# Loading a head's query and key stacks in eight transfers instead of twelve, and passing the row maxima through DRAM in three transfers instead of eight

## The chip, the cores and the metric

The kernel runs on one core of a Trainium2 chip. The metric is the device time of one execution in microseconds (us). Three runs of the kernel before took 3000.59, 3006.46 and 3000.59 us, a median of 3000.59 us.

## The reference: what is computed

Two multi-head attention blocks, A and B, read the same input `x` of 2048 tokens by 512 features. Each has 32 heads of 16 features, a full softmax over 2048 keys and an output projection. A gate per token mixes the two results.

```python
x = A_x
g = _sigmoid((x * gate_w).sum(-1, keepdims=True))
a = _A_ref(x, A_wqkv, A_wo)      # qkv projection, softmax(q k^T / 4) v per head, output projection
b = _B_ref(x, B_wqkv, B_wo)
return g * a + (1 - g) * b
```

So there are 64 heads in all (32 of A, then 32 of B), each with a 2048 by 2048 score matrix.

## The kernel before, in words

**Precision.** TensorE works on a rounded 32-bit type. To keep accuracy, a value is split into a rounded part ("hi") and the rest ("lo"), and a product is made from hi·hi + lo·hi + hi·lo. For the scores this is done by stacking: for head h, the tile `k_st` holds the 16 key rows as hi, lo, hi (48 partitions), and `q_st` holds the query rows as hi, hi, lo. One matrix product over these 48 partitions sums the three terms. Two more partitions of `q_st` (rows 48 and 49 of the stack) hold the row maximum of every query, split in two parts, and the same rows of `k_st` hold -1, so a product over 50 partitions gives score minus maximum. The whole stack is there twice, at partitions 0 and 64 (`HALVES`), so that two matrix products with different row groups can run side by side.

**Prologue** (about the first 304 us). The projections to q and k (`project_qk`, L192 to L199) write both parts of q and k of each group of eight heads to DRAM tensors `qd` and `kd` of shape [2 parts, 8 heads, 16, 2048]. `project_v` (L214 to L218) writes v to DRAM. The stacks of heads 0 and 1 are loaded here by the GpSimd (POOL) queue.

**Main loop** (L552 to L577). It has 1024 rounds: 64 heads of 16 key tiles of 128 keys. A round r of head h has two halves. In each half, TensorE makes:

- two score products of 128 keys by 512 queries (`scores`, L540), which ScalarE (ACT) turns into exponentials (L543);
- two products for the row maxima of a later head (`max_half`, L108), which VectorE (DVE) reduces over 1024 keys (L110); these are 20 rounds ahead of the scores (16 rounds and `LEAD` = 4);
- eight products with v for the round before (`attend`, L512), which add up in PSUM.

When the last maximum of a head is done (round 16h - 5), `max_split` joins the two half maxima (L120 on VectorE) and splits them in two parts on GpSimd (L121, L122). One round later (round 16h - 4), `max_rows` transposes the small tile in blocks of 32 by 32 on VectorE (L127, tile `mt`, 128 partitions of 32 values), and the SyncE (SP) queue carries it into rows 48 and 49 of both stacks of `q_st` (L131). Round 16h, the first round of head h, needs these rows.

`load_stacks(h + 2)` is issued on the SP queue at the start of round 16h (L559, L95, L96), into the buffer that head h - 1 has just finished with (three buffers). The first maximum products that read it are those of round 16h + 12.

Where a head ends, its sums leave PSUM through ScalarE (L529) and the SP queue (L530). After each group of eight heads the results are normalised and projected (`load_den` to `project_out`, L344 to L400), spread over the rounds of the next group by a table of due rounds (`at`, L452 to L497). The order of the work on each engine is the order of the program text; `tc.manual_schedule()` keeps it, and the framework adds the semaphore waits that the tiles' reads and writes need.

Of the kernel before, what the change touches and what calls it, by code (L numbers as in the profile page):

```python
# [23 lines left out]
F32 = mybir.dt.float32  # L24
# [9 lines left out]
S = 2048  # L34
DM = 512
H = 32
DH = 16
# [4 lines left out]
HG = H // NG  # L42
# [6 lines left out]
SC = 3 * DH  # L49
# [3 lines left out]
def gated_mha(ctx: ExitStack, tc: tile.TileContext, xT, x, wqkv_a, wo_a, wqkv_b, wo_b, gate_w, out):  # L53
    nc = tc.nc
# [6 lines left out]
    dram = ctx.enter_context(tc.tile_pool(name="dram", bufs=1, space=DRAM))  # L61
# [3 lines left out]
    kd = [[dram.tile([2, HG, DH, S], F32, name=f"kd{s}{g}") for g in range(NG)] for s in range(2)]  # L65
    vd = [dram.tile([S, H * 17], F32, name=f"vd{s}") for s in range(2)]
    od = [dram.tile([HG, NQ, 32, 512], F32, name=f"od{g}") for g in range(2 * NG)]
    rd = [dram.tile([HG, S], F32, name=f"rd{g}") for g in range(2 * NG)]

    ident = const.tile([P, P], BF, name="ident")  # L70
# [14 lines left out]
    def load_stacks(h, dma=None):  # L85
        dma = dma or nc.sync.dma_start
        s, hh = divmod(h, H)
        g, j = divmod(hh, HG)
        q, k = q_st[h % 3], k_st[h % 3]
        qs, ks = qd[s][g], kd[s][g]  # L90

        for b in HALVES:
            for i in range(3):
                r = slice(b + i * DH, b + (i + 1) * DH)
                dma(k[r].bitcast(F32), ks[i % 2, j])  # L95
                dma(q[r].bitcast(F32), qs[i // 2, j])  # L96

    mxp = {}

# [25 lines left out]
    def max_rows(h):  # L125
        mt = small.tile([P, 32], F32, name="mt")
        dve.transpose(mt, mparts.pop(h).rearrange("p i t -> p (i t)").bitcast(F32))  # L127
        q = q_st[h % 3]
        for b in HALVES:
            for a in range(4):  # L130
                nc.sync.dma_start(  # L131
                    q[b + SC:b + SC + 2].bitcast(F32).rearrange("i (t a x) -> i t a x", a=4, x=32)[:, :, a],
                    mt[32 * a:32 * a + 32])


    vpool = ctx.enter_context(tc.tile_pool(name="vpool", bufs=2))
# [10 lines left out]
    with tc.tile_pool(name="xs", bufs=1) as xs, tc.tile_pool(name="pro", bufs=2) as pro, \  # L147
# [98 lines left out]
        for i, (s, g, isk) in enumerate(blocks):  # L246
            block(split_w, i + 1)
            block(load_w, i + 3)
            if i in (2, 8):
                load_w(i // 8, 2 * DM, DM)  # L250
            if i in (4, 9):
                split_w(i // 8, 2 * DM, DM)
            project_qk(s, g, isk, lambda: run_ahead(i >= 10))
            if i in (7, 9):
                load_stacks((i - 7) // 2, pool.dma_start)
            if i == 7:
                for t in range(NT):
                    project_v(0, t)
            if i == 9:
                for c in range(4):  # L260
                    load_v(0, c)
        for t in range(NT):
            project_v(1, t)
            if pending:
                pending[0] += 1
                if pending[0] == 3:
                    max_rows(pending.pop() - 3)
            if t:
                run_ahead(2)
# [282 lines left out]
    for r in range(ROUNDS + 1):  # L552
        for fn, a in later.pop(r, ()):
            fn(*a)
        h, kt = divmod(r, NT)
        m = r + NT + LEAD
        if r < ROUNDS:
            if kt == 0 and h + 2 < NH:
                load_stacks(h + 2)  # L559
            pt[r] = ppool.tile([P, S], F32, name="p")  # L560
            for half in range(2):
                pair(r, (2 * half, 2 * half + 1))
                if m < ROUNDS:
                    max_half(m, half)
                elif fill and r >= fill[0][0]:
                    fill_in(r)
                if r:
                    attend(r - 1, half)
            if m < ROUNDS and m % NT == NT - 1:
                max_split(m // NT)  # L570
                after[r + 1] = m // NT
        else:
            attend(r - 1, 0)
            attend(r - 1, 1)
        if r in after:
            max_rows(after.pop(r))
        fill_in(r)  # L577
# [27 lines left out]
```

## Time and profile before

| | before |
|---|---|
| median of three runs | 3000.59 us |
| profiled execution | 3003.09 us |
| its span, first to last instruction | 3001.3 us |
| granted TensorE clock, mean | 0.994 |
| TensorE (PE) busy | 2962.8 us, 99% |
| VectorE (DVE) busy | 2678.3 us, 89% |
| ScalarE (ACT) busy | 2336.4 us, 78% |
| GpSimd (POOL) busy | 206.1 us, 7% |
| share of the chain that ended last on PE | 93% |
| transfers of `k_st` and `q_st` loads on the SP queue | 372 and 372, 128 KB each |
| transfers of `mt` into `q_st` on the SP queue | 512, 4 KB each |

The span is the time from the first to the last instruction. "Busy" counts the time in which an engine's instructions are recorded as running; matrix products overlap each other, so a PE that is always busy may still be held up, and the distance between the starts of two instructions says more than their durations. In the timeline a row gives start, duration, engine, line, operation, tile written and tiles read, shape and count. Transfers are issued by a queue (SPq, POOLq) and land later; a row's duration is that of issuing.

### The profile page before, as it was taken

What the parts mean: (1) busy time and instruction counts of PE and PEld (TensorE: products, weight loads), DVE (VectorE), ACT (ScalarE), POOL (GpSimd) and SP (SyncE); (2) the same over time, 40 slices, a digit from 0 to 9 for tenths busy, and PEclk for the clock granted to TensorE, in tenths of its full rate; (3) what the DMA queues carried; (4) which work ended last, traced back from release to release, by engine and by line L of the source; (5) the groups of instructions that cost most, each with busy time, mean ns of one, the idle gap of its engine ahead of it and who ended that gap; (6) DMA issues with size and microseconds to landing.
All of it is one profiled execution on the core that took longest, in us unless ns stands there. A gap on an engine that the chain in (4) does not pass through costs nothing.

```text
span 3001.3 us, 62628 instructions
## 1 busy us (share of the span) xinstructions
PE 2962.8 (99%) x26192; PEld 1207.5 (40%) x26192; DVE 2678.3 (89%) x2423; ACT 2336.4 (78%) x4277; POOL 206.1 (7%) x325
## 2 busy tenths in 40 slices
PE   8999999999999999999999999999999999999998
PEld 6877333333333333333333333333333333333334
DVE  3135999999999999999999999999999999999974
ACT  3221888888788878888788878888788878888893
POOL 2000222001000100001000100000000100000000
PEclk9999999999999999999999999999999999999998
DMA  8453444333333423343234432343334443343302
GB/s 254 184 199 120 79 76 77 55 60 53 56 59 52 77 41 54 55 81 48 44 55 66 66 53 40 55 81 51 53 47 63 65 62 47 45 76 51 55 12 81
DMA packets 94162, 213.65 MB, mean 71 GB/s; under 512 B 34552, under 2 KB 44760, under 8 KB 81592
## 3 DMA queue, kind: packets, MB, share of 16 engines
q1 hardware_dynamic: 90552, 197.58, 36.8%
q0 software_dynamic: 3328, 12.06, 1.4%
q8 instruction: 207, 3.39, 0.5%
q14 instruction: 75, 0.61, 0.1%
HBM read 143.78 MB, written 63.69 MB: 69 GB/s over the span
## 4 chain that ended last, share of the span: by engine, by line
PE 93%; ACT 3%; DMA 2%; issue 1%; DVE 0%; SPq 0%; ACTq 0%; DVEq 0%
PE acc L512 36%; PE ps_st L540 29%; PE ps_mx L108 16%; PE ps_pro L192 5%; PE ps_mx L395 4%; PE ps_pro L214 3%; ACT p L543 2%; ACT ev L529 1%; DMA q_st<-qd 1%; DMA qd<-part 1%; DMA kd<-part 0%; PE ps_mx L445 0%; DMA raw<-in_xT 0%; ACT o_hi L383 0%; DMA rb<-rd 0%
## 5 line engine op out<-in xcount | busy, mean ns | idle before, releaser
L543 ACT ACTIVATE p<-ps_st 128x512 f32<-128x512 f32 x4096 | 2223.5, 596 | 411.8 <-PE ps_st L540 189.3
L110 DVE TENSOR_REDUCE mxp<-ps_mx 128x1 f32<-128x1024 f32 x2048 | 2486.8, 1222 | 61.9 <-PE ps_mx L108 54.4
L512 PE MATMUL acc<-p,vg 128*17 128x256 f32 x16384 | 1287.5, 386 | 12.7 <-ACT ev L529 11.4
L540 PE MATMUL ps_st<-q_st,k_st 50*128 50x512 f32 x4096 | 1046.0, 497 | 5.3 <-ACT p L543 4.2
L108 PE MATMUL ps_mx<-k_st,q_st 48*128 48x512 f32 x4096 | 842.4, 395 | 0.0
L540 PEld LDWEIGHTS ps_st<-q_st,k_st 50*128 50x128 f32 x4096 | 395.2, 183 | 876.7 <-issue 484.0
L512 PEld LDWEIGHTS acc<-p,vg 128*17 128x17 f32 x16384 | 272.4, 95 | 752.9 <-issue 712.0
L108 PEld LDWEIGHTS ps_mx<-k_st,q_st 48*128 48x128 f32 x4096 | 403.5, 187 | 20.5 <-issue 16.4
L121 POOL CAST mparts<-mrow 128x16 fp32r<-128x16 f32 x64 | 12.6, 196 | 2031.6 <-DVE mrow L120 2031.6
L197 DVE TENSOR_TENSOR part<-ps_pro,part 128x1024 fp32r<-128x1024 f32 x32 | 39.2, 1224 | 119.6 <-ACT part L196 98.7
L196 ACT CAST part<-ps_pro 128x1024 fp32r<-128x1024 f32 x32 | 32.4, 1014 | 140.7 <-PE ps_pro L192 118.6
L400 DVE SCALAR_TENSOR_TENSOR o_acc<-ps_mx,gate,o_acc 128x512 f32<-128x512 f32 x112 | 83.8, 750 | 28.7 <-PE ps_mx L395 28.5
L192 PE MATMUL ps_pro<-xh,whi 128*128 128x512 f32 x256 | 73.4, 406 | 15.0 <-ACT xh L178 7.8
L217 ACT COPY v_st<-ps_pro 128x512 f32<-128x512 f32 x32 | 18.8, 586 | 80.5 <-PE ps_pro L214 80.5
L192 PE MATMUL ps_pro<-xh,wlo 128*128 128x512 f32 x256 | 70.3, 397 | 0.0
L192 PE MATMUL ps_pro<-xl,whi 128*128 128x512 f32 x256 | 69.8, 395 | 0.0
L395 PE MATMUL ps_mx<-wo_hi,o_hi 128*128 128x512 f32 (+1 forms) x128 | 65.0, 508 | 0.3 <-DVE o_acc L400 0.2
L192 PEld LDWEIGHTS ps_pro<-xh,whi 128*128 128x128 f32 x256 | 47.5, 191 | 30.5 <-ACT xh L178 10.1
L192 PEld LDWEIGHTS ps_pro<-xh,wlo 128*128 128x128 f32 x256 | 49.2, 192 | 10.6
L192 PEld LDWEIGHTS ps_pro<-xl,whi 128*128 128x128 f32 x256 | 49.2, 192 | 10.5
L166 DVE TENSOR_TENSOR wlo<-wraw,whi 128x512 fp32r<-128x512 f32 x16 | 10.9, 682 | 46.8 <-ACT whi L165 46.8
L395 PE MATMUL ps_mx<-wo_hi,o_lo 128*128 128x512 f32 (+1 forms) x128 | 51.6, 403 | 0.0
(73 smaller groups left out, 710.5 us busy)
## 6 DMA issues: line engine op xcount, KB each, us to landing
k_st<-kd SPq DMA_DIRECT2D x372, 128.0 KB
q_st<-qd SPq DMA_DIRECT2D x372, 128.0 KB
qd<-part SPq DMA_DIRECT2D x32, 512.0 KB
kd<-part SPq DMA_DIRECT2D x32, 512.0 KB
od<-ev SPq DMA_DIRECT2D x63, 256.0 KB
vd<-v_st SPq DMA_DIRECT2D x32, 272.0 KB
vg<-vd POOLq DMA_DIRECT2D x32, 272.0 KB, 3.7
q_st<-mt SPq DMA_DIRECT2D x512, 4.0 KB
```

The costliest lines, as they stand in the source:

```text
L108: pe.matmul(ps[:, c * 512:(c + 1) * 512], q[b:b + SC, t * P:(t + 1) * P], k[b:b + SC, o:o + 512], start=True, stop=True)
L110: dve.tensor_reduce(mxp[h][:, t, half:half + 1], ps, op=ALU.max, axis=AX.X)
L192: pe.matmul(ps[:, c * 512:(c + 1) * 512], a[:, k], b[:, k], start=n == 0, stop=n == 3 * KC - 1)
L196: act.copy(pt[0], ps)
L197: dve.tensor_tensor(pt[1], ps, pt[0].bitcast(F32), op=ALU.subtract)
L214: pe.matmul(ps[:, :DM], a[:, k, o:o + P], b[:, k], start=n == 0, stop=n == 3 * KC - 1)
L395: pe.matmul(ps[:, :DM], a[:n, sl], b[:n], start=i == 0, stop=i == 2)
L400: dve.scalar_tensor_tensor(o_acc[:, t], ps[:, :DM], g, o_acc[:, t], op0=ALU.mult, op1=ALU.add)
L512: pe.matmul(acc[32 * c:32 * c + 17, half * 256:(half + 1) * 256], v[:, 4 * a + c if final else kt, j], p[:, o:o + 256], start=first and ha ...
L529: act.copy(ev, acc)
L540: pe.matmul(ps[:, i * 512:(i + 1) * 512], k[b:b + SC + 2, kk * P:(kk + 1) * P], q[b:b + SC + 2, cc * 512:(cc + 1) * 512], start=True, stop ...
L543: act.activation(pt[r][:, o:o + n], ps[:, :n], AF.Exp, scale=SCALE)
```

## The change

```diff
+    md = [dram.tile([2, S], F32, name=f"md{i}") for i in range(3)]
...
+        def pairs(t, step):
+            v = t[0, j]
+            return bass.AP(tensor=v.tensor, offset=v.offset, ap=[[S, DH], [step, 2], [1, S]])
+
         for b in HALVES:
-            for i in range(3):
-                r = slice(b + i * DH, b + (i + 1) * DH)
-                dma(k[r].bitcast(F32), ks[i % 2, j])
-                dma(q[r].bitcast(F32), qs[i // 2, j])
+            dma(k[b:b + 32].bitcast(F32), pairs(ks, HG * DH * S))
+            dma(q[b:b + 32].bitcast(F32), pairs(qs, 0))
+            dma(k[b + 32:b + 48].bitcast(F32), ks[0, j])
+            dma(q[b + 32:b + 48].bitcast(F32), qs[1, j])
...
         q = q_st[h % 3]
+        r = md[h % 3]
+        nc.sync.dma_start(r.rearrange("i (t a x) -> a (i t) x", a=4, x=32), mt)
         for b in HALVES:
-            for a in range(4):
-                nc.sync.dma_start(
-                    q[b + SC:b + SC + 2].bitcast(F32).rearrange("i (t a x) -> i t a x", a=4, x=32)[:, :, a],
-                    mt[32 * a:32 * a + 32])
+            nc.sync.dma_start(q[b + SC:b + SC + 2].bitcast(F32), r)
```

**Stacks.** The first 32 rows of each stack are now interleaved: row 2d of `k_st` is the hi part of feature d and row 2d + 1 its lo part; in `q_st` both rows are the hi part (a step of 0 in the source reads it twice). One transfer of 256 KB loads such 32 rows; the last 16 rows (hi keys, lo queries) take a transfer of 128 KB as before. The same 1.5 MB are loaded per head, in eight transfers (four per stack) instead of twelve. Each product still multiplies the same pairs of rows; they only stand in another order among the partitions.

**Row maxima.** `mt` went straight from SBUF to SBUF, in eight transfers of 4 KB, four for each stack. Now one transfer of 16 KB writes all of `mt`, put in order by its destination pattern, to a small DRAM tensor `md` (three of them, in turn), and two transfers of 16 KB each read `md` into the two rows of the lower and the upper stack. The reads wait on the SP queue until the write has landed.

## The prediction

> **What bounds the kernel now.** First the page: engines' shares, the chain, the costliest groups.
>
> ```profile
> PE 2962.8 (99%) x26192; PEld 1207.5 (40%) x26192; DVE 2678.3 (89%) x2423; ACT 2336.4 (78%) x4277; POOL 206.1 (7%) x325
> ...
> PE 93%; ACT 3%; DMA 2%; issue 1%; DVE 0%; SPq 0%; ACTq 0%; DVEq 0%
> ...
> L110 DVE TENSOR_REDUCE mxp<-ps_mx 128x1 f32<-128x1024 f32 x2048 | 2486.8, 1222 | 61.9 <-PE ps_mx L108 54.4
> ...
> L540 PE MATMUL ps_st<-q_st,k_st 50*128 50x512 f32 x4096 | 1046.0, 497 | 5.3 <-ACT p L543 4.2
> ```
>
> TensorE holds 93% of the chain, transfers 2%. If "PE busy" meant TensorE at its peak, moving transfers about could give nothing. But durations of overlapping products hide hold-ups, so I measure each half-round from the start of its score pair (L540) to the start of the next. I lay windows between those starts for 48 heads: heads 1 to 62 without those whose window falls into the output projection of a finished group. First the eighth round of each head, an ordinary one (first and last window, sum over all 48):
>
> ```profile
> 364.31:365.53 1.22, 1.22 (x16) 1.00 0.00 0
> ...
> 2893.73:2894.94 1.21, 1.21 (x16) 1.00 0.00 0
> sum 58.58, PE 58.58; mean PE 1.22
> ```
>
> The same for the first half of round 16h, where the row maxima are first needed:
>
> ```profile
> 346.72:348.15 1.43, 1.43 (x16) 1.00 1.28 317
> ...
> 2876.29:2877.66 1.37, 1.37 (x17) 1.00 0.04 12
> sum 69.59, PE 69.25; mean PE 1.44
> ```
>
> And for the first half of round 16h + 12, where the stack of head h + 2 is first read (48 heads from 0 to 61, with the same kind left out):
>
> ```profile
> 336.49:338.16 1.67, 1.67 (x16) 1.00 0.00 0
> ...
> 2866.15:2867.73 1.58, 1.58 (x16) 1.00 0.00 0
> sum 76.06, PE 76.02; mean PE 1.58
> ```
>
> So TensorE, "busy" throughout and at a granted clock of 1.00, loses 69.59 - 58.58 = **11.0 us** at the first place and 76.06 - 58.58 = **17.5 us** at the second. The change touches both. Their causes follow from one head, its timeline on TensorE, VectorE and the SP queue:
>
> ```profile
> 911.85 0.20 DVE L127 STREAM_TRANSPOSE mt<-mparts 128x32 f32<-128x32 f32 x1
> 912.08 5.27 SPq L131 DMA_DIRECT2D q_st<-mt  x8
> 917.22 0.50 PE L540 MATMUL ps_st<-q_st,k_st 50*128 50x512 f32 x2
> 917.75 0.31 SPq L95 DMA_DIRECT2D k_st<-kd  x1
> 918.43 0.62 PE L540 MATMUL ps_st<-q_st,k_st 50*128 50x512 f32 x2
> ...
> 924.47 0.42 SPq L96 DMA_DIRECT2D q_st<-qd  x1
> 926.37 0.34 SPq L530 DMA_DIRECT2D od<-ev  x1
> ...
> 947.96 0.50 PE L540 MATMUL ps_st<-q_st,k_st 50*128 50x512 f32 x2
> 948.30 0.75 PE L108 MATMUL ps_mx<-k_st,q_st 48*128 48x512 f32 x2
> ...
> 949.88 0.40 PE L108 MATMUL ps_mx<-k_st,q_st 48*128 48x512 f32 x2
> ```
>
> Place one: issuing the eight small transfers lasts until 912.08 + 5.27 = 917.35, and the pair at 918.43 runs 0.62 instead of 0.50, because its second product starts late. That it waits for transfers, the instructions of L540 in a later head's boundary (996 to 999 us) show: four waiting instructions stand in TensorE's sequencer, and one lasts 685 ns.
>
> ```profile
> L540 PEldq EVENT_SEMAPHORE  x4: 51/51/685, 996.7 to 997.5; - x4
> ```
>
> Place two: the loads were issued by 924.9, 23 us before 947.96. Nothing is late there. But the pair of L108 takes 0.75 instead of 0.40, and the same view of L108 shows six waiting instructions, none of which waits long:
>
> ```profile
> L108 PEldq EVENT_SEMAPHORE  x6: 51/51/51, 947.9 to 948.5; - x6
> ```
>
> Twelve transfers loaded this stack, so six instructions carry two waits each, about (948.5 - 947.9) / 5 = 0.12 us apart. The first three hide behind the score pair (the L108 pair starts 0.34 after it, as ever); the last ones push its second product out.
>
> **The change part by part.**
>
> *Row maxima.* Eight issues (5.27 us) and a landing go. In their place stands a chain of write, wait, two reads. For small transfers through DRAM in a quiet stretch the chain of waits near the end has both links, each from issue to landing:
>
> ```profile
> 2917.84 2.00 DMA od<-ev
> ...
> 2919.89 2.51 DMA dn<-od
> ...
> 2927.14 7.15 DMA rb<-rd
> ```
>
> I take 2.0 for the write and 2.5 for a read, as nearest rows. Before the second read (upper stack) stands the first one's issue, 0.4 to 0.6 by the SP rows (0.42 for the stack rows, 5.27 / 8 = 0.66 for the small ones). Sum: 2.0 + 2.5 + 0.6 = 5.1 us. Available are 918.43 - 912.08 = 6.35 us. So the rows land about 1.2 us early and place one returns to 1.22: **-11.0 us**. Both ends: nothing saved if the chain takes the 6.5 us of now, and a loss beyond, if a read costs 7.15, the largest in that fence (rivals). What waits on the SP queue behind the blocked reads is load_stacks, then od<-ev; the queue is free again at about 912.08 + 2.0 + 1.2 = 915.3 instead of 917.35, so nobody is later.
>
> [...]
>
> *Stacks.* Same bytes, four fewer transfers per head. On the SP queue this is off the path: loads have from 924.9 to 947.96, so even the 256 KB transfers at twice the issue time cost nothing; if that cover were gone, the cost would be a pair waiting at round 16h + 12. In the prologue POOL issues 16 instead of 24:
>
> ```profile
> L95 POOL DMA_DIRECT2D k_st<-kd x12: 484/484/683, 39.3 to 63.6; - x12
> L96 POOL DMA_DIRECT2D q_st<-qd x12: 484/484/501, 39.9 to 64.5; - x12
> ...
> L108 PE MATMUL ps_mx<-k_st,q_st x4096: 385/388/628, 180.1 to 2905.0; 48*128 48x512 f32 x196
> ```
>
> They go out by 65 us and are read first at 180.1: nothing. What counts is place two: eight transfers to wait for make four waiting instructions of six. Two fewer at 0.12 take 0.24 off the end of the string; since the starts are rounded I take 0.21 of the 17.5 / 48 = 0.36 us: 48 x 0.21 = **-10 us**. Ends: 0, if the number of waits isn't what holds the pair, and -17.5, if all four hide.
>
> *Does another engine cap this?* The busy times of TensorE, its weight loads, VectorE, ScalarE and GpSimd in the half-round from 917.22, and VectorE's timeline at place two, where L120 stands between the reduces, and L127 a round later:
>
> ```profile
> 917.22:918.43 1.21, 1.21 (x16) 0.43 (x12) 1.21 (x2) 1.08 (x3) 0.00 (x0) 1.00 0.04 7
> ...
> 948.78 0.17 DVE L120 TENSOR_TENSOR mrow<-mxp 128x16 f32<-128x16 f32 x1
> 949.09 2.45 DVE L110 TENSOR_REDUCE mxp<-ps_mx 128x1 f32<-128x1024 f32 x2
> 951.47 0.20 DVE L127 STREAM_TRANSPOSE mt<-mparts 128x32 f32<-128x32 f32 x1
> 951.59 3.64 DVE L110 TENSOR_REDUCE mxp<-ps_mx 128x1 f32<-128x1024 f32 x3
> ```
>
> ScalarE has room, 1.08 of 1.21. VectorE seems to have none. But the transpose starts at 951.47, before the recorded end of the reduce (949.09 + 2.45 = 951.54). So a record is at least 0.07 longer than the reduce holds VectorE, and over 32 reduces it can catch up 2 us a head: no cap, I think.
>
> **Sum:** -11 - 10 = **-21 us**. The profiled execution took 3003.09 (span 3001.3 and 1.8 around it), so its counterpart is 2982; it lies 2.5 above the median of the runs, 3000.59, from which I forecast **2980 us**.
>
> **The rivals.**
>
> *One of the two gains only: about 2990.* VectorE's records may be right: then its idle time caps the gain, 949.09 - (948.78 + 0.17) = 0.14 us at place two and, by the pair's 0.62 instead of 0.50, 0.12 at place one: 48 x 0.26 = 12 us. Or the waits don't fall in number (-11), or the maxima arrive just as late as now (-10). For it: a reduce of 1222 ns mean leaves no idle time. Against: the transpose that starts early.
>
> *The reads of long rows land late: slower, about 3030.* Each read moves two rows of 8 KB. The rows most like it are the stack loads of the prologue, 8 KB to each partition:
>
> ```profile
> DMA to landing us min/median/max: 7.3/9.3/11.1
> ```
>
> The kernel becomes slower when the chain passes 6.35 + 0.23 (today's hold-up, 11.0 / 48) + 0.21 (place two's gain), some 6.8 us. With a read half way between 2.51 and 7.15, 4.8, it takes 2.0 + 4.8 + 0.6 = 7.4, so TensorE stands 1.05 us in 48 heads: +50 - 11 - 10 = +29. Against: those loads ran twelve at a time, while the last half-round ahead of 918.43 has a DMA share of 0.04 at 7 GB/s (row above).
>
> [...]
>
> *The change does nothing: 3000.* The new chain lands when the old one did and the waits are hidden or as many as now. Against: 5.1 to 6.35.
>
> **How the numbers follow.** Forecast 0.60, one gain only 0.20, nothing 0.08, late reads 0.08, a slow write 0.04. A measurement of this kernel can tell 0.2%, 6 us, from no change; so faster 0.80, same 0.08, slower 0.12. The likeliest case's own range: both places fully healed, -28.5 (2972), to -14 (2987) if the waits count only in proportion (4/12 of 17.5 is 6) and some heads stay late. To hold 8 in 10 the range adds the one-gain case and a run that lies as high as the 3006.46 did: 2969 to 2998. Outside lie the slower cases and most of no change.
>
> **What would show it.** Right: in the boundary's timeline one L131-like write near the transpose, two reads some 2 us later, the score pair at 16h back to 0.50; the windows' means 1.22 and about 1.37; at round 16h + 12 four waiting instructions of L108. Wrong: waiting instructions of L540 of a microsecond or more at round 16h (chain too long); means unchanged at place two with four waits (the count isn't the cause); or VectorE's idle at L110 gone with half-rounds longer than 1.22 elsewhere (VectorE caps).

## The result and the profile after

The changed kernel takes 2977.22 us (median of four runs, 2973.93 to 2981.99) against 3002.13 us for the kernel before in the same session: a ratio of 0.9921, 95% interval 0.9908 to 0.9933. That is 24.9 us faster; the forecast was 2980. The interval of the ratio leaves 20 to 28 us for the gain.

The page of the changed kernel, with the rows that answer to those of before (lines have moved: L540 is now L544, L108 is L113, L110 is L115):

```profile
PE 2936.9 (99%) x26192; PEld 1193.4 (40%) x26192; DVE 2673.4 (90%) x2423; ACT 2336.3 (79%) x4277; POOL 202.3 (7%) x317
...
PE 92%; ACT 3%; DMA 3%; issue 1%; DVE 1%; SPq 0%; ACTq 0%; DVEq 0%
...
L115 DVE TENSOR_REDUCE mxp<-ps_mx 128x1 f32<-128x1024 f32 x2048 | 2484.7, 1222 | 47.5 <-PE ps_mx L113 45.7
...
L544 PE MATMUL ps_st<-q_st,k_st 50*128 50x512 f32 x4096 | 1034.7, 497 | 6.4 <-ACT p L547 5.7
```

TensorE is "99% busy" as before, although its busy time fell by 26 us. The share says nothing here: the hold-ups were inside the busy time, as the prediction read it. What shows them are the windows from one score pair to the next, laid as in the prediction over the same 48 heads. For the changed kernel, in this order: the ordinary eighth round; the first half of round 16h (the maxima's first use, "place one"); the first half of round 16h + 12 (a stack's first use, "place two"). Each is the last window and the sum:

```profile
2870.61:2871.82 1.21, 1.21 (x16) 1.00 0.00 0
sum 58.61, PE 58.61; mean PE 1.22
...
2853.35:2854.57 1.22, 1.22 (x18) 1.00 0.05 13
sum 58.62, PE 58.62; mean PE 1.22
...
2843.42:2844.79 1.37, 1.37 (x18) 1.00 0.00 0
sum 65.95, PE 65.95; mean PE 1.37
```

Place one went from 69.59 to 58.62 us, an ordinary half-round; place two from 76.06 to 65.95. Together that is 21.1 us.

One head in the timelines of VectorE, the SP queue and TensorE:

```profile
903.19 0.20 DVE L132 STREAM_TRANSPOSE mt<-mparts 128x32 f32<-128x32 f32 x1
903.42 0.59 SPq L135 DMA_DIRECT2D md<-mt  x1
905.41 0.52 SPq L137 DMA_DIRECT2D q_st<-md  x2
909.08 0.56 SPq L98 DMA_DIRECT2D k_st<-kd  x1
909.77 0.50 PE L544 MATMUL ps_st<-q_st,k_st 50*128 50x512 f32 x2
...
939.38 0.50 PE L544 MATMUL ps_st<-q_st,k_st 50*128 50x512 f32 x2
939.72 0.53 PE L113 MATMUL ps_mx<-k_st,q_st 48*128 48x512 f32 x2
```

The waiting instructions of the maximum products (L113) between 938.8 and 941 us, with their shortest, median and longest time in ns:

```profile
L113 PEldq EVENT_SEMAPHORE  x4: 51/51/51, 939.3 to 939.7; - x4
```

The write is issued 0.03 us after the transpose, the reads 1.99 us after the write, and the score pair at 909.77 lasts 0.50: nobody waits for the maxima. At place two four waiting instructions stand where there were six, and the pair of L113 lasts 0.53 instead of 0.75.

The profiled executions lie 28.6 us apart, more than the medians. Of these, 3.8 us lie before the first score product, which starts at 300.7 instead of 304.5 us (the prologue, below). Another 19.3 us lie between it and the first score product of the last head (at 2914.6 us before, at 2891.4 after), and 5.5 us behind that.

The 19.3 us are less than the 21.1, since some 1.9 us are lost again right behind place one. In seven heads (10, 18, 26 and so on to 58) ScalarE converts the output of a finished group of heads just there, and TensorE, which now comes earlier, waits for ScalarE instead. The half-round behind place one grows in these seven heads from 1.60 to 1.88 us on average; in the others it stays. In head 10 of the changed kernel:

```profile
698.04 1.05 ACT L387 CAST o_hi<-num 128x1024 fp32r<-128x1024 f32 x1
...
699.64 0.50 PE L544 MATMUL ps_st<-q_st,k_st 50*128 50x512 f32 x1 [0.17 <-ACT p L547]
```

The 5.5 us at the end come from a stretch in which TensorE stands for 2.85 us before and 3.10 us after ahead of a score product that waits for ScalarE (in the chain of before the read `rb<-rd`, 7.15 us, stands ahead of it), and then runs at half clock for a while. Before and after, windows with the granted clock in the third column from the right:

```profile
2939.00:2963.00 24.00, 24.00 (x99) 0.51 0.06 24
```

```profile
2915.00:2925.00 10.00, 9.54 (x37) 0.50 0.00 2
```

How long this stretch lasts (24 us here, 10 there) is not set by the kernel alone. The run e8 below has the instructions of the changed kernel, and from the first score product of its last head to the end it takes 85.4 us, against 81.2 in the changed kernel's profile and 86.7 before. The mean clock differs between runs of one kernel, too: the four runs of the changed kernel have 0.997 (2974.47 and 2973.93 us) and 0.995 (2981.99 and 2979.97). So I don't count these 5.5 us to the change. The recorded busy time doesn't show the half rate here: TensorE is busy for 24.00 of the 24 us and for 9.54 of the 10.

### The profile page after: what moved, and what is told of

The parts are those of the page before. It is cut to its first block, busy times and chain, and to the rows that moved or that the text cites. A ratio compares the mean times of both kernels' runs of the same rounds, so it can differ in the third digit from the quotient of the medians.

```text
span 2972.7 us, 61649 instructions
## 1 busy us (share of the span) xinstructions
PE 2936.9 (99%) x26192; PEld 1193.4 (40%) x26192; DVE 2673.4 (90%) x2423; ACT 2336.3 (79%) x4277; POOL 202.3 (7%) x317
## 4 chain that ended last, share of the span: by engine, by line
PE 92%; ACT 3%; DMA 3%; issue 1%; DVE 1%; SPq 0%; ACTq 0%; DVEq 0%
PE acc L516 36%; PE ps_st L544 28%; PE ps_mx L113 15%; PE ps_pro L196 5%; PE ps_mx L399 4%; PE ps_pro L218 3%; ACT p L547 2%; ACT ev L533 1%; DMA k_st<-kd 1%; DMA kd<-part 1%; DMA raw<-in_xT 0%; DMA rb<-rd 0%; PE ps_mx L449 0%; DMA qd<-part 0%; ACT o_hi L387 0%
## 5 line engine op out<-in xcount | busy, mean ns | idle before, releaser
L115 DVE TENSOR_REDUCE mxp<-ps_mx 128x1 f32<-128x1024 f32 x2048 | 2484.7, 1222 | 47.5 <-PE ps_mx L113 45.7
L544 PE MATMUL ps_st<-q_st,k_st 50*128 50x512 f32 x4096 | 1034.7, 497 | 6.4 <-ACT p L547 5.7
L113 PE MATMUL ps_mx<-k_st,q_st 48*128 48x512 f32 x4096 | 822.7, 394 | 0.0
L544 PEld LDWEIGHTS ps_st<-q_st,k_st 50*128 50x128 f32 x4096 | 387.0, 183 | 875.2 <-issue 482.4
L113 PEld LDWEIGHTS ps_mx<-k_st,q_st 48*128 48x128 f32 x4096 | 398.2, 187 | 12.1 <-issue 9.0
```

The source lines that it names most:

```text
L113: pe.matmul(ps[:, c * 512:(c + 1) * 512], q[b:b + SC, t * P:(t + 1) * P], k[b:b + SC, o:o + 512], start=True, stop=True)
L115: dve.tensor_reduce(mxp[h][:, t, half:half + 1], ps, op=ALU.max, axis=AX.X)
L544: pe.matmul(ps[:, i * 512:(i + 1) * 512], k[b:b + SC + 2, kk * P:(kk + 1) * P], q[b:b + SC + 2, cc * 512:(cc + 1) * 512], start=True, stop ...
```

## The experiments

All kernels were timed beside the kernel before, whose median was 3001.9, 3001.6 and 3001.9 us in the three sessions. For each, place one and place two are the sums of the 48 windows in us, and the last column is the start of the first score product in us, from one profiled execution each.

| run | time, us | ratio to before [95%] | place one | place two | first score product |
|---|---|---|---|---|---|
| before | 3002.1 | | 69.59 | 76.06 | 304.5 |
| the change | 2977.2 | 0.9921 [0.9908, 0.9933] | 58.62 | 65.95 | 300.7 |
| e1, stacks only | 2991.1 | 0.9968 [0.9957, 0.9979] | 74.37 | 65.87 | 299.2 |
| e2, maxima only | 2994.4 | 0.9975 [0.9963, 0.9987] | 58.71 | 76.80 | 306.1 |
| e3, sixteen loads throughout | 3001.4 | 0.9996 [0.9985, 1.0006] | 58.62 | 86.84 | 300.3 |
| e4, maxima a round later | 2996.7 | 0.9982 [0.9973, 0.9991] | 76.13 | 65.75 | 300.3 |
| e7, prologue loads on SP | 2982.0 | 0.9934 [0.9914, 0.9954] | 58.57 | 66.10 | 302.3 |
| e6, four loads, prologue as e7 | 2975.0 | 0.9917 [0.9894, 0.9940] | 58.60 | 58.89 | 306.1 |
| e9, prologue loads spread | 2971.8 | 0.9899 [0.9882, 0.9915] | 58.60 | 66.11 | 296.6 |
| e12, four loads, spread | 2967.1 | 0.9882 [0.9868, 0.9897] | 58.67 | 58.94 | 298.4 |

### One part of the change alone

e1 is the kernel before with the new `load_stacks`; e2 is the changed kernel with the old one:

```diff
 # e2
-            dma(k[b:b + 32].bitcast(F32), pairs(ks, HG * DH * S))
-            ...
+            for i in range(3):
+                r = slice(b + i * DH, b + (i + 1) * DH)
+                dma(k[r].bitcast(F32), ks[i % 2, j])
+                dma(q[r].bitcast(F32), qs[i // 2, j])
```

> Only the stack loads are changed (eight transfers); the maxima go straight from SBUF to SBUF in eight transfers as before. My theory (place one waits for the last of the eight small transfers, place two for the number of waits; the two are independent): the mean first half-round of a head stays at 1.44 us, the half-round 16h + 12 falls from 1.58 to 1.37 us, the first score product comes near 300.7 us as in the changed kernel instead of 304.5, and the time is 3002 - 10 - 4 = 2988 us. Rival (the gain comes from a lighter SP queue as a whole, so that the first half-round heals too): first half-round below 1.30 us and about 2980 us. Rival (VectorE caps): half-round 16h + 12 not below 1.45 us, 2993 us or more.

> Only the maxima go through DRAM in three transfers; the stacks are loaded in twelve transfers as before. My theory: first half-round 1.22 us, half-round 16h + 12 stays at 1.58 us, first score product near 304.5 us (the prologue is that of before), time 3002 - 11 = 2991 us. Rival (lighter SP queue): the half-round 16h + 12 falls below 1.50 us too, 2985 us or less.

The sums over the 48 windows, place one and then place two, of e1 and of e2:

```profile
sum 74.37, PE 73.06; mean PE 1.52
...
sum 65.87, PE 65.87; mean PE 1.37
```

```profile
sum 58.71, PE 58.71; mean PE 1.22
...
sum 76.80, PE 76.74; mean PE 1.60
```

Each place follows its own part: the maxima heal place one (58.71) and leave place two (76.80), the stacks heal place two (65.87). The lighter queue as a whole doesn't do it. But my "independent" was too strong. In e1 place one didn't stay at 69.59, it grew to 74.37, by 4.8 us or 0.10 per head. One head of e1:

```profile
902.10 0.20 DVE L131 STREAM_TRANSPOSE mt<-mparts 128x32 f32<-128x32 f32 x1
902.33 5.35 SPq L135 DMA_DIRECT2D q_st<-mt  x8
908.68 0.77 PE L544 MATMUL ps_st<-q_st,k_st 50*128 50x512 f32 x2
```

In the same head before, the eight were issued in 5.27 us and the pair lasted 0.62; the transpose stood 6.58 us ahead of the pair, as it does here. So it is only in part that TensorE now comes too early. Over the 48 heads, round 16h starts 0.22 us sooner after place two, but the transpose moves with it by 0.18, and this leaves 0.04 of the 0.10 us. The other 0.06 is that the eight transfers end later after the transpose. Why their issue takes longer in e1 is not shown. Either way, 4.8 of the 10.2 us saved at place two are lost at place one, and only with the short way of the maxima does the whole saving of the stacks stay. The times, 2991.1 and 2994.4 us, lie 3 us above what I had expected of each. Alone, the parts give 10.8 and 7.5 us; together 24.9, so here the whole is more than the sum of its parts. At the two places alone it is 5.4 and 10.1 us against 21.1.

### Is it the number of waits at place two?

e3 cuts each load in two, with the same bytes and rows:

```diff
-            dma(k[b:b + 32].bitcast(F32), pairs(ks, HG * DH * S))
...
+            for x in range(n):          # n = 2
+                lo, w = b + x * 16, 32 // n
+                dma(k[lo:lo + w].bitcast(F32), half(pairs(ks, HG * DH * S), n, x))
...                                      # likewise the other three loads
```

> The changed kernel with each of the eight loads of the main loop cut in two (sixteen transfers of 128 or 64 KB, the same bytes and rows; the prologue keeps eight). My theory (the half-round 16h + 12 is held by the number of waiting instructions, some 0.105 us each): eight waiting instructions instead of four, the half-round grows from 1.36 to about 1.78 us, 48 x 0.42 = 20 us more than the changed kernel, about 2997 us; the first half-round stays at 1.22 us. Rival (landing or bytes count, not the number): half-round 16h + 12 stays near 1.36 us and the time near 2977 us.

One thing differs from that text: POOL's loads in the prologue were cut in two as well, so this run has sixteen throughout. The waiting instructions at one head's place two:

```profile
L123 PEldq EVENT_SEMAPHORE  x8: 51/51/51, 942.1 to 942.9; - x8
```

And the sum of the 48 windows there:

```profile
sum 86.84, PE 86.46; mean PE 1.80
```

Eight instructions, and place two rises by 86.84 - 65.95 = 20.9 us, 0.435 per head, where 0.42 had been expected. Nothing landed late: each waiting instruction took 51 ns. e6 and e12 go the other way, below. Over 2, 4, 6 and 8 waiting instructions the half-round at place two lasts 1.23, 1.37, 1.58 and 1.81 us on average. The first two hide behind the score pair; each pair of further ones costs 0.15, then 0.21, then 0.22 us. The time of e3, 3001.4 us, lies 4 us above what I had expected of it.

### How much room the maxima have

e4 moves the transpose and the transfers one round later:

```diff
-                after[r + 1] = m // NT
+                after[r + 2] = m // NT
```

> The changed kernel with transpose and transfers of the maxima one round (2.43 us) later, so that 6.35 - 2.43 = 3.9 us remain for the write, the wait and the reads. The profile of the changed kernel gives 4.4 us from the issue of the write to the landing of the second read. My theory: TensorE stands 0.5 us or a little more in the first half-round of the 48 heads, mean first half-round about 1.75 us, 48 x 0.5 = 24 us more, about 3001 us. With the 5.1 us of the forecast's sum it would be 1.2 us, mean 2.4 us, about 3035 us. Rival (the maxima's way is not what the first half-round hangs on): 1.22 us and 2977 us.

The sum at place one:

```profile
sum 76.13, PE 75.79; mean PE 1.58
```

The SP queue and TensorE at one head:

```profile
908.15 0.59 SPq L135 DMA_DIRECT2D md<-mt  x1
910.14 0.52 SPq L137 DMA_DIRECT2D q_st<-md  x2
...
912.35 0.80 PE L544 MATMUL ps_st<-q_st,k_st 50*128 50x512 f32 x2 [0.20 <-DMA q_st<-md]
```

TensorE now waits for the read by name, 0.20 us for the lower stack, and its pair lasts 0.80 instead of 0.50. From the write's issue at 908.15 to 912.35 + 0.30 = 912.65 are 4.5 us; that is the length of the chain as its user feels it. Place one costs 76.13 - 58.62 = 17.5 us and the time rises by 19.5. That is a little under the 24 of my theory, and far from the 57 that the forecast's 5.1 us would have given. So the maxima in the changed kernel are some 1.9 us early, not 1.2.

### The prologue

The first score product came 3.8 us earlier after the change, where the forecast had said nothing would come of the prologue. e8, meant to have sixteen prologue loads, had eight and so only repeats the changed kernel: 2980.75 us in one run, first score product at 299.8 us. e10 puts twelve loads into the prologue only.

> The changed kernel with sixteen transfers instead of eight for each of the stacks of heads 0 and 1 in the prologue only. My theory (POOL keeps eight transfers under way; smaller ones drag the loads out and with them the stores that TensorE waits for): the loads are issued until some 75 us instead of 57, the first score product comes 4 us or more later than in the changed kernel, at 304 us or later. Rival (the four microseconds between the prologues of before and after are scatter): first score product near 300 us.

> The changed kernel with twelve loads for each of heads 0 and 1 in the prologue only. If the prologue's three to four microseconds belong to these loads, POOL starts them near 39.3 us, TensorE's busy time between 40 and 75 us falls from 31.6 to 28 to 30 us as in the two runs with twelve, and the first score product comes near 303 to 306 us. If they were scatter: 31.6 and 300 us.

TensorE's busy time between 40 and 75 us, before; in the changed kernel; in e10:

```profile
40.00:75.00 35.00, 28.25 (x123) 1.00 1.03 267
```

```profile
40.00:75.00 35.00, 31.60 (x131) 0.95 1.04 307
```

```profile
40.00:75.00 35.00, 29.39 (x128) 1.00 1.03 270
```

The twelve loads bring the stand back, and the first score product to 303.9 us. (The time of e10 in its one run is 2974.8 us, no longer than that of the changed kernel: the prologue's part is seen in the trace and is too small to be seen in the times.) So this part of the gain belongs to the prologue's loads: with twelve 304.5, 306.1 and 303.9 us, with eight 300.7, 299.2, 300.3 and 299.8, from one profiled execution of each kernel. In the chain of waits of the changed kernel the stores of q and k are what TensorE hangs on there:

```profile
42.56 10.43 DMA qd<-part
...
54.33 15.41 DMA kd<-part
```

These stores stand beside the loads in transfers that are busy to the full (the last column but one, the DMA share, is 1.03 to 1.04). That alone doesn't make TensorE stand: in e12 below the share is 1.03 as well, and TensorE is busy for all 35.00 us. Why twelve hold the stores longer than eight (15.20 and 14.31 us before, together 29.5 against 25.8) I could not settle. With twelve, POOL starts its first load at 39.3 to 39.8 us (before, e2, e10) instead of 41.3 (the changed kernel), since that load needs only the hi part. e11 takes this lead away:

```diff
-                for i in range(3):
+                for i in (1, 0, 2):
```

> As the run with twelve loads in the prologue, but each stack's lo keys are loaded first, so that the first load has to wait for the store of the lo part and POOL starts near 41.3 us, as it does with eight. If it is the start two microseconds earlier that puts the loads ahead of the first store of q: TensorE's busy time between 40 and 75 us near 31.6 us and the first score product near 300 us. If it is the number of the loads: 28 to 30 us and 303 us or later.

POOL then started at 41.8 us, yet TensorE's busy time stayed at 30.00 us and the first score product came at 308.2 us (2979.2 us in its one run): not the earlier start. The number alone isn't it either, for e3 has sixteen, 32.44 us and 300.3 us. This stays open.

What does help is to take the loads out of the crowd. e7 moves them to the SP queue, head 0's in a lump behind the eighth projection block and head 1's behind the tenth; e9 spreads them:

```diff
 # e9
+        early = load_stacks(0) + load_stacks(1)      # sixteen pieces
+        share = len(early) // 8
...
+        def between(i):                              # after each half of a block
+            if 3 <= i < 7:
+                for _ in range(share):
+                    nc.sync.dma_start(*early.pop(0))
+            run_ahead(i >= 10)
```

> The changed kernel with the stack loads of heads 0 and 1 on the SP queue after the eighth projection block, where they come when the first stores of q and k are long done, instead of on the POOL queue, where they start at 41 us among these stores. My theory for the prologue (these loads crowd the stores, TensorE stands some 3.4 us between 42.5 and 71.1 us): the stores land in some 3 us, the first score product comes at about 297 us instead of 300.7, about 2974 us. Rival (the stores are slow for another reason, or the SP queue holds something up later): first score product at 300 us or later, no gain.

> The changed kernel with the eight loads each of heads 0 and 1 spread singly over the projection blocks 4 to 7 of the prologue, two after each half block, on the SP queue. My theory (whatever stores come right behind a crowd of stack loads land late and hold TensorE): without a crowd no store is late, TensorE's stand of some 3.4 us between 40 and 75 us goes and doesn't come back later, first score product at 297 us, 2974 us or a little less. Rival (the stretch is short of transfer bandwidth with or without a crowd): TensorE stands as long elsewhere, first score product at 300 us or later.

TensorE's windows in e7 and in e9, 40 to 75 and 100 to 200 us:

```profile
40.00:75.00 35.00, 35.00 (x156) 1.00 0.67 241
...
100.00:200.00 100.00, 94.54 (x408) 0.98 0.65 200
```

```profile
40.00:75.00 35.00, 35.00 (x156) 1.00 0.90 278
...
100.00:200.00 100.00, 99.33 (x434) 1.00 0.51 186
```

The lump only moves the stand: none between 40 and 75 us, but 5.5 us between 100 and 200, where the stores of v come right behind it. My theory's sign was right for the first place and its sum wrong: first score product at 302.3 us, no gain. Spread, the loads hold TensorE for 0.67 us at most in these two stretches: first score product at 296.6 us, and 2971.8 us in all.

### Four loads: a version faster than both

```diff
-    qd = [[dram.tile([2, HG, DH, S], ...
+    qd = [[dram.tile([3, HG, DH, S], ...            # kd too
...
-                for i in range(2):                  # project_qk
+                for i, p in enumerate((0, 1, 0) if isk else (0, 0, 1)):
                     nc.sync.dma_start(dst[i]..., pt[p].bitcast(F32))
...
+            ap=[[S, DH], [HG * DH * S, 3], [1, S]]  # a stack's 48 rows in one transfer
+            dma(k[b:b + SC].bitcast(F32), threes(ks))
+            dma(q[b:b + SC].bitcast(F32), threes(qs))
```

> The changed kernel with three parts of q and k stored in the prologue (the doubled hi part is written twice, half as many stores again), so that one transfer of 384 KB loads a stack of 48 rows: four transfers per head in place of eight. The loads of heads 0 and 1 go out on the SP queue after the eighth projection block. My theory (the waits at 16h + 12): two waiting instructions instead of four, both hidden behind the score pair, the half-round falls from 1.36 to about 1.22 us, 48 x 0.15 = 7 us less; with up to 3 us in the prologue about 2968 us, the fastest of all. Rival (the added stores cost TensorE time in the prologue): first score product later than 303 us, no gain or a loss in all.

> The kernel with three stored parts and four loads per head, its loads of heads 0 and 1 spread one by one over the projection blocks 4 to 7. My theory: the half-round 16h + 12 stays at 1.22 us as in the run with four loads, and the prologue no longer pays, first score product at 300 us or earlier; 2977 - 7 = 2970 us or less, the fastest. Rival (the added stores themselves cost TensorE time): first score product at 304 us or later, about 2974 us.

In e12, the waiting instructions at one head's place two:

```profile
L115 PEldq EVENT_SEMAPHORE  x2: 51/51/51, 932.4 to 932.5; - x2
```

And the sum of the 48 windows:

```profile
sum 58.94, PE 58.94; mean PE 1.23
```

Place two is gone in both (58.89 and 58.94). In e6 the rival held for the prologue: with the added stores and the lump of loads the first score product comes at 306.1 us (302.3 in e7, which has the lump alone), and the gain in time is small (2975.0). With the loads spread (e12) it is 298.4 us, and the kernel takes 2967.1 us, 0.9882 of before. That is the fastest median of all, clear of the changed kernel's (0.9908 at the least); from e9 it isn't told apart, since the two intervals overlap.

## Why the prediction was right

**The sum.** Forecast 11.0 + 10 = 21 us in the loop; measured 10.97 at place one (69.59 to 58.62) and 10.11 at place two (76.06 to 65.95). That 0.21 us per head comes off place two was right to the hundredth: (76.06 - 65.95) / 48 = 0.21. The reason, the number of waiting instructions, is shown by e3, e6 and e12; the hundredth is luck, for the 0.24 of two waits was brought down to 0.21 for rounded starts, and no row gave the size of that step. Over the whole loop the gain was 19.3 us.

**The chain through DRAM.** The step that put 2.0 us on the write was right (1.99 from issue to the reads' issue). The read was sized too long: 2.5 plus 0.6 for the issue ahead of it. Two reads are issued in 0.52 us together, 0.26 each, and the whole chain is 4.5 us instead of 5.1 (e4), which leaves 4.5 - 1.99 - 0.26 = 2.25 for a read. The margin was larger than forecast; the sum didn't depend on it. A write that takes twice as long because of its small pieces, to which 0.04 had been given, is shown by no run: the 16 KB write in pieces of 128 bytes takes the 2.0 us that the 256 KB store of `ev` took (2.00). One of the arguments against the rivals was misread, and no term hung on it: the prologue's loads do not run twelve at a time. Before, POOL issues eight, until 44.1 us, and then waits 4.63 us for one to land.

**VectorE as a cap.** Not reached: its idle time ahead of L115 fell from 61.9 to 47.5 us, and the two places gained 21.1 us where the rival allowed 12. That the recorded length of a reduce is longer than it holds the engine was the right reading: in the changed kernel, too, a transpose starts 0.08 us before the recorded end of the reduces ahead of it (903.19 against 900.83 + 2.44).

**ScalarE.** The prediction read its room, 1.08 of 1.21 us, from an ordinary half-round. Behind place one of seven heads there is none, and this is the 1.9 us by which the loop gained less than its two places.

**What was wrong.** "They go out by 65 us and are read first at 180.1: nothing." This step asked only who reads the loads, not who stands beside them. The stores of q and k share the transfers' time with them (a DMA share of 1.03 and 1.04), and TensorE waits for these stores: 3.8 us between the profiles, and the stand comes back in e10. It would be about the difference between 21 us forecast and 24.9 measured, but that isn't shown: 21 lies within the interval of the measured gain, the loop gave 1.9 us less than its two places, and e10 was not slower. That the forecast came within 3 us is in part luck, since these two errors have opposite signs.

**What would have been missed.** The two terms were added as if independent. e1 shows they aren't: without the short way of the maxima, 4.8 us of the stacks' gain would have been lost at place one.

## What to carry to other kernels

An engine at 99% can hide stalls inside its records (28.5 us at two places here); the distance between the starts of like instructions, averaged over like places, shows them and sizes each one. Where many transfers feed one matrix product, count the waits and not only the landings: fewer, larger transfers took 0.21 us per two waiting instructions off TensorE although the transfers had been issued 23 us before. And when bulk transfers are called hidden, ask who else needs the transfers at that moment: the loads were hidden, the stores beside them weren't (3.8 us between the profiles here).

## What the runs showed that I had not expected

A transfer of 16 KB in 128-byte pieces to DRAM and back costs 4.5 us as its user feels it, less than eight direct transfers of 4 KB one after the other (5.27 us to issue them alone).

Cutting time at one place moved another that had looked unrelated: in e1 the mean at place one rose from 1.45 to 1.55 us a head although nothing there was changed (74.37 against 69.59 us over the 48 heads), more than half of it because the same eight transfers ended later.

Eight, twelve and sixteen loads per head of the same bytes in the prologue gave first score products at 299 to 301, 304 to 308 and 300 us. Neither their number nor their start explains it, and it stays open.
